# Projecting two z2 row blocks inside the last four segments of a memory-transformer and gMLP kernel

## The chip, the core and the metric

The kernel runs on one NeuronCore of a Trainium2 chip. The core has a matrix engine (TensorE, PE), which writes its results to PSUM, a vector engine (VectorE, DVE), a scalar engine (ScalarE, ACT), a general engine (GpSimd, POOL), and a queue engine (SyncE, SP), which here only issues transfers. The engines run at the same time and wait for each other through semaphores. The metric is the time of one execution on the device in microseconds, the median over several executions.

## The reference

Two parts follow each other on a sequence of 2048 tokens with 512 features. The first is attention with a recurrent memory, in segments of 32 tokens (64 segments), each with 8 memory tokens that come out of the segment before. The second is a gated MLP (gMLP).

```python
for s in range(n_seg):                      # 64 segments, one after the other
    h = concatenate([mem, x_norm[segment]]) # 8 + 32 tokens
    q, k, v = h @ Wq, h @ Wk, h @ Wv        # 32 heads of 128
    o = softmax(q @ k.T * scale + mask) @ v
    o = o @ Wo
    mem = o[:, :8]; outs.append(o[:, 8:])
h = x + concatenate(outs)

z  = gelu(layernorm(h) @ w_in)              # 512 -> 1792
z1 = z[..., :896]
z2 = layernorm(z[..., 896:])
g  = w_sp @ z2 + b_sp                       # mixing over the 2048 tokens
out = h + (z1 * g) @ w_out
```

The weights are bf16, and so is the output.

## The kernel before

**Order.** Every operation is recorded in program order by a small emitter (`em.add`), which derives the semaphore waits from named tokens for what an operation reads and writes. Each engine then runs its own operations strictly in that order; there is no scheduler. A token `("ps", b)` stands for one of the eight PSUM banks.

**The recurrence** is the loop over `s` from line 913. In a segment TensorE projects q, k and v (`QK`, `V_half`; the matmuls are recorded by the helper `mm` at L289 and L290), scores them (`S_half`), ACT computes the exponentials, the logarithm and the reciprocal (`sm_exp` L608, `sm_ln` L626, `sm_rcp` L630), DVE normalises (`sm_norm` L634), TensorE multiplies with V (`PV_half`, L666 and L672), ACT and DVE copy the result out (`cT_evac`, L686 and L688), and TensorE multiplies with Wo (`Wo`, L701). ACT copies that to `part` (`part_evac`, L713), and `mem_out` (L722, L728, L730) turns its first 8 rows into the memory of the next segment. `mask_dve` (L585) puts the mask into PSUM once a segment on DVE.

Matmuls with 32 tokens use only 32 columns of the array. They are issued in groups of four, in four column tiles (`tile_position=(0, 32 * c)`), which run at the same time; the profile writes such a matmul as 128*32.

**Filler places.** There are two lists of work that doesn't depend on the segment in hand. `gx` has groups of five steps: four with four matmuls each (one for each 128 of the 512 features) into PSUM bank 3 (`XB`), and one that copies the result out. Each segment takes one group (line 999). Two steps stand ahead of `PV_half`, two behind it, and the copy stands behind the copies of `cT`:

```python
        fill(nw1)
        for f in xs[:2]:
            f()
        PV_half(s, 0)
        PV_half(s, 1)
        for f in xs[2:4]:
            f()
        fill(nw2)
        cT_evac(0, "act", (0,))
```

`gx` holds 60 groups, for keys, queries and values of later memory rows, and so the segments 60 to 63 have none. The other list, `wq`, holds the output projection of the memory rows of the four segments before (`WoX_mm`, L751), and the sums `F_group` (L736) and `WoX_scatter` (L761), which put the rows of four segments together in one block of 128 tokens. Where a segment has a group of `gx`, `wq` gives `nw1` pieces ahead of it and none in the middle; where it has none, it gives one ahead and the others in the middle.

**Where the recurrence ends.** After segment 63 the loop over `rb` from line 1167 makes the gMLP's inputs, one block of 128 tokens at a time. For each block, `z2_mm` projects two halves of 448 columns (`HF`) with four matmuls each (L1108), and ACT applies GELU from PSUM (L1111). `z2_norm` and `z2_apply` normalise on DVE and POOL (L1121 to L1132). From block 2 on, two groups of z1 are projected in each block (`z1_group`, L1139), with GELU on ACT (L1142), and from block 4 on five matmuls of the mixing (`mix`, L1146). The PSUM banks 5 to 7 go round through `zbank()`.

Into the first blocks the rest of the recurrence is woven: the last `F_group(15)` between the halves of block 0, 32 matmuls `WoX_mm` behind it, `WoX_evac` (L756) on ACT, and `WoX_scatter`, `F_add` (L741) and `h_done` in block 1. `F_add(14)`, the same sum for the block before, is the last operation of the loop over segments on DVE. `xn2_apply` (L774) normalises the token blocks 14 and 15 in the blocks 1 and 2, and TensorE transposes them (L1190) in the blocks 2 and 3, with a copy by DVE (L1104).

**Transfers around it.** SP issues them in order: in segments 48 to 51 the second half of `w_in` (`w_in2`), from segment 49 on the transposed token blocks (`xn2T_dma`), in segment 63 the first 512 tokens of the mixing weights (`load_wT(0)`, L907), then the first half of `w_in` (`w_in1`, L974), the bias (L975) and six transposed blocks (L788); behind them `h_done`'s store (L771), more mixing weights, `w_out`, and the 16 blocks of h.

Of the kernel before, what the change touches and what calls it, by code (L numbers as in the profile page):

```python
# [9 lines left out]
ACT = mybir.ActivationFunctionType  # L10
# [168 lines left out]
def fast_path(nc, st, keep, A_x, A_mem0, A_Wq, A_Wk, A_Wv, A_Wo, A_seg_len, B_w_in, B_w_sp, B_b_sp, B_w_out, out):  # L179
# [8 lines left out]
    RB = S // 128  # L188
    DC = D // 128
    F = B_w_in.shape[1]  # L190
    FH = F // 2
# [15 lines left out]
    def sb(name, shape, dt):  # L207
        return st.enter_context(nc.sbuf_tensor("f_" + name, shape, dt))
# [5 lines left out]
    def region(off, n):  # L214
        return arena[:, off:off + n]
# [21 lines left out]
    Vs = sb("Vs", [128, 2, 512], BF)  # L237
# [5 lines left out]
    xn = sb("xn", [128, 2, 512], BF)  # L243
# [28 lines left out]
    ps = st.enter_context(nc.psum_tensor("f_ps", [128, 8, 512], F32))  # L272
# [5 lines left out]
    def PB(b):  # L278
        return ("ps", b)

    def sp(fn, **k):
        return em.add("sp", fn, dma=True, **k)

    def pe(fn, **k):
        return em.add("pe", fn, **k)
# [9 lines left out]
    def act(fn, **k):  # L295
        return em.add("act", fn, **k)

    def dve(fn, **k):
        return em.add("dve", fn, **k)
# [234 lines left out]
    XB = 3  # L534
# [198 lines left out]
    def F_group(rb, bank):  # L733
        for j in range(4):
            i = (4 * rb + j) % 8
            pe(lambda e, i=i, j=j: e.matmul(ps[32 * j:32 * j + 32, bank, :], lhsT=F_sb[:, :], rhs=part[:, i, :], start=True, stop=False,  # L736
                                            tile_position=(0, 32 * j)),
               reads=[("part", i, 0), ("part", i, 1), "F"], writes=[PB(bank)])

    def F_add(rb, bank):  # L740
        dve(lambda e: e.tensor_tensor(out=hbuf[:, rb % 2, :], in0=ps[:, bank, :], in1=hbuf[:, rb % 2, :], op=ALU.add),  # L741
            reads=[PB(bank), ("h", rb % 2)], writes=[("h", rb % 2)])
# [4 lines left out]
    def WoX_mm(rb, qr, bgs=range(8)):  # L747
        for bg in bgs:
            b, g = bg // 4, bg % 4
            h = 16 * b + 4 * qr + g  # L750
            pe(lambda e, h=h, g=g, i=8 * qr + bg: e.matmul(ps[32 * g:32 * g + 32, WXB, :], lhsT=cTx[:, rb % 2, i, :], rhs=w_o[:, h, :],  # L751
                                                           start=(i < 4), stop=(i >= H - 4), tile_position=(0, 32 * g)),
               reads=[("cTx", rb % 2), ("Wo", h // 8)], writes=[PB(WXB)])

    def WoX_evac(rb):
        act(lambda e: e.activation(out=partx[:], in_=ps[:, WXB, :], func=ACT.Copy), reads=[PB(WXB)], writes=["partx"])  # L756

    def WoX_scatter(rb, bank):
        for c in range(4):
            q = slice(32 * c, 32 * c + 32)  # L760
            pe(lambda e, q=q, c=c: e.matmul(ps[q, bank, :], lhsT=Sc[:, q], rhs=partx[:], start=False, stop=True, tile_position=(0, 32 * c)),  # L761
               reads=["partx", "Sc"], writes=[PB(bank)])
# [10 lines left out]
    def xn2_apply(rb, j):  # L773
        dve(lambda e: e.tensor_scalar(out=xo[:, j, :], in0=hbuf[:, rb % 2, :], scalar1=mv[:, rb, 0:1], scalar2=rstd[:, rb:rb + 1],  # L774
                                      op0=ALU.subtract, op1=ALU.mult),
            reads=[("h", rb % 2), ("mv", rb), ("rstd", rb)], writes=[("xo", j)])
# [5 lines left out]
    w_in2 = region(4 * WSZ, WH).rearrange("p (dc f) -> p dc f", dc=DC)  # L782
    w_in1 = region(4 * WSZ + QX, WH).rearrange("p (dc f) -> p dc f", dc=DC)
    xts = [region(4 * WSZ + i * QX + WH, 8 * D).rearrange("p (r dc t) -> p r dc t", r=8, dc=DC) for i in range(2)]
# [94 lines left out]
    gx = []  # L879
# [7 lines left out]
    for ck in range(1, 4):  # L887
        for n in range(4 if ck == 1 else 0, 8):
            vx_group(ck, n)
        for r in range(4):  # L890
# [2 lines left out]
                    qkx_group(ck, mi, r, b)  # L893


    wTb = [region(0, RB * 512).rearrange("p (t sc c) -> p t sc c", sc=RB, c=64),
           region(3 * WSZ, RB * 512).rearrange("p (t sc c) -> p t sc c", sc=RB, c=64)]
    h_sb = region(RB * 512, RB * D).rearrange("p (rb d) -> p rb d", rb=RB)
# [2 lines left out]
    z2 = region(2 * WSZ, RB * FH).rearrange("p (rb f) -> p rb f", rb=RB)  # L901
# [3 lines left out]
    def load_wT(tb, after):  # L905
        for t in range(8):
            sp(lambda e, t=t: e.dma_start(wTb[tb % 2][:, t, :, :], wT_d[8 * tb + t]), reads=[("wTd", 8 * tb + t)],  # L907
               writes=[("wT", tb % 2, t)], after=after)
# [4 lines left out]
    for s in range(NSEG):  # L913
        j4 = s % 4
        rb = s // 4
# [154 lines left out]
        if 3 * CK <= s < 3 * CK + 4:  # L1070
            dc = s - 3 * CK
# [7 lines left out]
    lastQ, lastK, lastV = lastop["q"], lastop["k"], lastop["v"]  # L1079
# [1 line left out]

    TB = 512
    NTB = S // TB
    HF = FH // 2
    em.mark_const("w_in1", "w_out", *[("w_in2", dc) for dc in range(DC)])

    def xT2(rb):
        return xts[rb // 8][:, rb % 8, :, :]
# [13 lines left out]
    def xn_copy(rb, j, bank):  # L1102
        src = psb[:, bank, 0:512].rearrange("p (dc c) -> p dc c", dc=DC)
        dve(lambda e: e.tensor_copy(out=xT2(rb), in_=src), reads=[PB(bank)], writes=[("xn2T", rb)], after=[lastop["s"], lastop["x"]])  # L1104

    def z2_mm(rb, hf, bank):
        for dc in range(DC):
            pe(lambda e, dc=dc: e.matmul(ps[:, bank, 0:HF], lhsT=xT2(rb)[:, dc, :], rhs=w_in2[:, dc, hf * HF:(hf + 1) * HF],  # L1108
                                         start=(dc == 0), stop=(dc == DC - 1)),
               reads=[("w_in2", dc), ("xn2T", rb)], writes=[PB(bank)])  # L1110
        act(lambda e: e.activation(out=z2[:, rb, hf * HF:(hf + 1) * HF], in_=ps[:, bank, 0:HF], func=ACT.Gelu_apprx_tanh),  # L1111
            reads=[PB(bank)], writes=[("z2", rb, hf)], after=[lastV])

    st2 = sb("st2", [128, 2, 2, 6], F32)
    mv2 = sb("mv2", [128, 2, 2], F32)
# [2 lines left out]
    def z2_norm(rb):  # L1118
        j = rb % 2
        for hf in range(2):  # L1120
            dve(lambda e, hf=hf: e.bn_stats(out=st2[:, j, hf, :], in_=z2[:, rb, hf * HF:(hf + 1) * HF]), reads=[("z2", rb, hf)],  # L1121
                writes=[("st2", j, hf)])
# [36 lines left out]
    def zbank():  # L1159
        zcnt[0] += 1  # L1160
        return 5 + zcnt[0] % 3
# [3 lines left out]
    ACC = (0, 1, 2, 3, 4)  # L1165
    LAG = 4
    for rb in range(RB):
        z2_mm(rb, 0, zbank())
        if rb == 0:
            F_group(RB - 1, XB)  # L1170
        z2_mm(rb, 1, zbank())
        if rb == 0:
            for qr in range(4):
                WoX_mm(RB - 1, qr)
            endA = em.by_eng["pe"][-1]
            WoX_evac(RB - 1)
            load_wT(1, [endA])
            sp(lambda e: e.dma_start(w_out, B_w_out.rearrange("(fb p) d -> p fb d", p=128)), writes=["w_out"], after=[endA])
        if rb == 1:
            WoX_scatter(RB - 1, XB)  # L1180
            F_add(RB - 1, XB)
            h_done(RB - 1)
            for r in range(RB):
                sp(lambda e, r=r: e.dma_start(h_sb[:, r, :], h_d[r]), reads=[("hd", r)], writes=[("hs", r)], after=[lastQ])
        if rb in (1, 2):
            xn2_apply(RB - 3 + rb, rb % 2)
        if rb in (2, 3):
            r, j, bank = RB - 4 + rb, (rb - 1) % 2, zbank()
            for dc in range(DC):
                pe(lambda e, dc=dc, j=j, bank=bank: e.transpose(out=psb[:, bank, dc * 128:(dc + 1) * 128], in_=xo[:, j, dc * 128:(dc + 1) * 128],  # L1190
                                                                identity=ident[:, :]), reads=[("xo", j), "ident"], writes=[PB(bank)])
            xn_copy(r, j, bank)
        z2_norm(rb)
        if rb > 0:
            z2_apply(rb - 1)
        for _ in range(2):
            if rb >= 2 and z1list and (z1list[0][0] < 3 or rb >= 12):
                tb, fb = z1list.pop(0)
                z1_group(tb, fb, zbank())
        if rb == 8:  # L1200
            check_rows()
        if rb >= LAG:
            for fb, bk in enumerate(ACC):
                mix(0, fb, rb - LAG, bk)
# [33 lines left out]
    for tb in range(NTB):  # L1238
        for fb in range(len(ACC) if tb == 0 else 0, FB):
            if tb == 0:  # L1240
                bank = 5 + fb % 3
            else:
                bank = MB[mcnt % 3]
# [19 lines left out]
    for d0 in (0, 256):  # L1263
        bank = 7 if d0 else 5
# [9 lines left out]
def general_path(nc, st, keep, A_x, A_mem0, A_Wq, A_Wk, A_Wv, A_Wo, A_seg_len, B_w_in, B_w_sp, B_b_sp, B_w_out, out):  # L1274
# [23 lines left out]
    if True:  # L1298
# [51 lines left out]
        def PB(b):  # L1350
            return ("ps", b)
# [423 lines left out]
        if True:  # L1775
# [24 lines left out]
            wspr = B_w_sp.rearrange("(tk p) s -> p tk s", p=128)  # L1800
            HF = FH // 2
            tstate = {"cnt": 0, "banks": (4, 5)}
# [40 lines left out]
            def z2_mm(rb, hf):  # L1843
                bank = 2 + hf
                for dc in range(DC):
                    em.add("pe", lambda e, dc=dc: e.matmul(
                        ps[:, bank, 0:HF], lhsT=xn2T[:, dc, rb * 128:(rb + 1) * 128], rhs=w_in[:, dc, FH + hf * HF:FH + (hf + 1) * HF],
                        start=(dc == 0), stop=(dc == DC - 1)),
                        reads=["w_in", ("xn2T", rb)], writes=[PB(bank)])

            def z2_gelu(rb, hf):
                bank = 2 + hf
                em.add("act", lambda e: e.activation(
                    out=z2[:, rb, hf * HF:(hf + 1) * HF], in_=ps[:, bank, 0:HF], func=ACT.Gelu_apprx_tanh),
                    reads=[PB(bank)], writes=[("z2", rb)])
# [175 lines left out]
```

The softmax here doesn't subtract the row's maximum and nothing guards it: scores larger than these inputs give would overflow.

## Time and profile before

| what | us |
|---|---|
| median of 5 executions | 856.29 |
| lowest and highest | 855.45, 858.59 |
| the profiled execution, its own time | 856.26 |
| its span, from the first to the last instruction | 854.5 |

The mean granted TensorE clock of the profiled execution is 0.998. Its span in four stretches, as the view by stretches of time gives them (busy us of each engine):

| stretch, us from the start | what runs | PE | DVE | ACT | POOL |
|---|---|---|---|---|---|
| 607.73 to 617.46 | segment 57, with a filler | 9.71 | 5.93 | 6.60 | 1.69 |
| 646.64 to 656.37 | segment 61, without | 9.11 | 5.32 | 6.13 | 1.69 |
| 675.85 to 693.34 | end of the recurrence, first gMLP blocks | 16.77 | 12.49 | 10.69 | 5.28 |
| 693.34 to 852.50 | the rest | 156.34 | 70.69 | 25.71 | 11.28 |

In the profile, L and a number is a line of the kernel before. A row of the timeline has the start, the length, the engine, the line, the operation, what it writes and reads, and in brackets how long the engine had been idle and which operation it waited for. The ends of matmuls are modelled, so the distance between two starts says more than the length of one row. The copies of the mask, L585, come once a segment and serve as a mark for how long a segment takes.

### The profile page before, as it was taken

The page shows a single profiled execution, that of the slowest core. Times are in us where ns is not written, and L with a number is a line of the kernel's source. Part 1 is how long each engine was busy: PE and PEld are TensorE (multiplying, and loading weights), DVE is VectorE, ACT ScalarE, POOL GpSimd, SP SyncE. Part 2 cuts the span into 40 slices and gives each one's busy share as a digit, 9 for nine tenths or more (in the row PEclk, how much of TensorE's full clock was granted, in tenths as well). Part 3 has the DMA queues.
Part 4 walks back from the last instruction along what each step waited for, and adds up shares of the span by engine and source line. Part 5 has one row for each costly group of instructions (what it writes and reads, how often), then busy time and mean ns, then how long its engine had stood idle before and what let it go on. Part 6 is the DMA issues. An engine that isn't in the chain of part 4 may idle for free.

```text
span 854.5 us, 45967 instructions
## 1 busy us (share of the span) xinstructions
PE 836.1 (98%) x22497; PEld 440.9 (52%) x19432; DVE 513.3 (60%) x1318; ACT 472.4 (55%) x1367; POOL 169.0 (20%) x425
## 2 busy tenths in 40 slices
PE   8889999999999999999999999999999999999997
PEld 8545555555555555555555555555455444444443
DVE  3446666676766666666767666666666554453443
ACT  3446666766667666667666676766676655400000
POOL 7312212121211122121212111212112232100000
PEclk9999999999999999999999999999999999999999
DMA  9972222222332222312223423343321780033001
GB/s 324 390 218 77 68 66 35 60 72 60 77 91 64 42 65 42 78 34 60 68 63 77 91 62 73 74 78 80 60 48 50 205 265 1 1 111 107 30 13 41
DMA packets 112922, 75.27 MB, mean 88 GB/s; under 512 B 70728, under 2 KB 98512, under 8 KB 112720
## 3 DMA queue, kind: packets, MB, share of 16 engines
q1 hardware_dynamic: 111504, 70.88, 30.8%
q8 instruction: 166, 2.72, 1.4%
q0 software_dynamic: 384, 1.05, 0.3%
q10 hardware_dynamic: 832, 0.33, 0.1%
q14 instruction: 36, 0.29, 0.1%
HBM read 39.46 MB, written 20.58 MB: 70 GB/s over the span
## 4 chain that ended last, share of the span: by engine, by line
PE 92%; SPq 3%; DMA 2%; DVE 1%; issue 1%; ACT 1%; ACTq 0%
PE f_ps L289 33%; PE f_ps L701 14%; PE f_ps L290 12%; PE f_ps L1146 11%; PE f_ps L751 3%; PE f_ps L666 3%; PE f_ps L1220 3%; PE f_ps L1108 3%; PE f_ps L1139 3%; PE f_ps L498 2%; SPq L329 2%; DMA f_arena<-in_A_Wk_dram 2%; PE f_ps L595 1%; PE f_ps L615 1%; PE f_ps L672 1%
## 5 line engine op out<-in xcount | busy, mean ns | idle before, releaser
L289 PE MATMUL f_ps<-f_arena,f_hT 128*32 128x512 bf16 (+1 forms) x5632 | 360.4, 331 | 0.2
L289 PEld LDWEIGHTS f_ps<-f_arena,f_hT 128*32 128x32 bf16 x5632 | 134.9, 96 | 160.2 <-issue 69.4
L290 PE MATMUL f_ps<-f_arena,f_hT 128*32 128x512 bf16 (+1 forms) x2560 | 189.2, 315 | 0.0
L559 ACT ACTIVATE f_Tst<-f_ps 128x512 bf16<-128x512 f32 (+1 forms) x320 | 149.6, 510 | 57.7 <-PE f_ps L289 54.1
L701 PE MATMUL f_ps<-f_arena,f_cT 128*32 128x256 bf16 x4096 | 131.7, 276 | 1.4 <-ACT f_cT L686 0.8
L638 POOL TENSOR_TENSOR f_E_sb<-f_R_sb,f_E_sb 128x64 bf16<-128x64 f32 x128 | 57.0, 445 | 361.6 <-ACT f_R_sb L630 361.6
L567 DVE STREAM_TRANSPOSE f_QT<-f_Tst 128x256 uint32<-128x256 uint32 x128 | 57.0, 446 | 94.8 <-ACT f_Tst L559 94.8
L701 PEld LDWEIGHTS f_ps<-f_arena,f_cT 128*32 128x32 bf16 x4096 | 91.2, 95 | 38.4 <-ACT f_cT L686 22.1
L1146 PE MATMUL f_ps<-f_arena 128*128 128x512 bf16 x448 | 100.6, 379 | 0.0
L688 DVE TENSOR_SCALAR f_cT<-f_ps 128x160 bf16<-128x160 f32 x256 | 65.1, 316 | 35.7 <-PE f_ps L672 35.7
L713 ACT ACTIVATE f_part<-f_ps 128x256 bf16<-128x256 f32 x128 | 49.2, 384 | 60.0 <-PE f_ps L701 56.0
L658 DVE TENSOR_SCALAR f_V_sb<-f_ps 128x512 bf16<-128x512 f32 (+1 forms) x128 | 71.0, 555 | 13.7 <-PE f_ps L289 13.7
L686 ACT ACTIVATE f_cT<-f_ps 128x160 bf16<-128x160 f32 x256 | 57.1, 309 | 36.8 <-PE f_ps L672 36.8
L1146 PEld LDWEIGHTS f_ps<-f_arena 128*128 128x128 bf16 x448 | 43.8, 98 | 52.7
L567 DVE STREAM_TRANSPOSE f_KT<-f_Tst 128x128 uint32<-128x128 uint32 (+1 forms) x192 | 65.8, 356 | 2.7
L626 ACT ACTIVATE f_R_sb<-f_ps 128x160 f32<-128x160 f32 x128 | 39.0, 305 | 34.8 <-PE f_ps L290 32.9
L634 DVE TENSOR_TENSOR f_E_sb<-f_R_sb,f_E_sb 128x160 bf16<-128x160 f32 x128 | 41.6, 325 | 23.4 <-ACT f_R_sb L630 23.4
L1152 DVE TENSOR_TENSOR f_arena<-f_ps,f_arena 128x512 f32<-128x512 f32 x28 | 19.3, 690 | 54.4 <-PE f_ps L1146 52.4
L289 PE MATMUL f_ps<-f_arena,f_hTe 128*32 128x512 bf16 x640 | 48.8, 382 | 0.0
L608 ACT ACTIVATE f_E_sb<-f_ps 128x224 bf16<-128x224 f32 x128 | 45.8, 358 | 0.0
L751 PE MATMUL f_ps<-f_arena,f_cTx 128*32 128x512 bf16 x512 | 43.8, 379 | 0.0
L630 ACT ACTIVATE f_R_sb<-f_R_sb 128x160 f32<-128x160 f32 x128 | 42.6, 333 | 2.0
(117 smaller groups left out, 1024.6 us busy)
## 6 DMA issues: line engine op xcount, KB each, us to landing
wT_d<-f_wst SPq DMA_DIRECT2D x32, 256.0 KB
f_arena<-wT_d SPq DMA_DIRECT2D x32, 256.0 KB
f_arena<-in_A_Wv_dram SPq DMA_DIRECT2D x4, 1024.0 KB
f_arena<-in_A_Wk_dram SPq DMA_DIRECT2D x4, 1024.0 KB
f_arena<-in_A_Wo_dram SPq DMA_DIRECT2D x4, 1024.0 KB
f_Vx<-vext_d SPq DMA_DIRECT2D x124, 32.0 KB
f_arena<-in_A_Wq_dram SPq DMA_DIRECT2D x3, 1024.0 KB
vext_d<-f_Vs SPq DMA_DIRECT2D x20, 128.0 KB
```

Of the source, the lines that this page charges most:

```text
L289: return e.matmul(out, lhsT=lhsT, rhs=rhs, start=start, stop=stop, skip_group_check=True, tile_position=pos)
L290: return e.add_instruction(mybir.InstMatmult(name=nc.get_next_instruction_name(), engine=mybir.EngineType.PE, ins=[e.lower_ap(rhs), e.lowe ...
L559: act(lambda e: e.activation(out=st_.rearrange("p (hp i r) -> p hp i r", i=32, r=2), in_=ps[:, bank, 0:64 * np_].rearrange("p (hp r i) -> ...
L567: dve(lambda e: e.transpose(out=dst, in_=src), reads=tok, writes=[(nm, b, k) for k in halves(b, p0, np_)])
L638: pool(lambda e: e.tensor_tensor(out=ev, in0=rv, in1=ev, op=ALU.mult), reads=[("R", b), ("Ex", b)], writes=[("Ex", b)])
L658: dve(lambda e: e.tensor_scalar(out=dst, in0=src, scalar1=VSC, scalar2=None, op0=ALU.mult), reads=[PB(bank)], writes=tok)
L686: act(lambda e: e.activation(out=dst, in_=src, func=ACT.Copy, scale=UNSC), reads=[PB(PVB[c])], writes=tok)
L688: dve(lambda e: e.tensor_scalar(out=dst, in0=src, scalar1=UNSC, scalar2=None, op0=ALU.mult), reads=[PB(PVB[c])], writes=tok)
L701: pe(lambda e, h=h, g=g, i=i, b=b, c=c: e.matmul(ps[32 * g:32 * g + 32, bank, 0:d1 - d0], lhsT=cTh[:, i, 8:40], rhs=w_o[:, h, d0:d1], star ...
L713: act(lambda e: e.activation(out=part[:, s % 8, d0:d1], in_=ps[:, bank, 0:d1 - d0], func=ACT.Copy), reads=[PB(bank)], writes=[("part", s % ...
L751: pe(lambda e, h=h, g=g, i=8 * qr + bg: e.matmul(ps[32 * g:32 * g + 32, WXB, :], lhsT=cTx[:, rb % 2, i, :], rhs=w_o[:, h, :], start=(i < 4 ...
L1146: pe(lambda e: e.matmul(ps[:, bank, 0:TB], lhsT=z2[:, sc, fb * 128:(fb + 1) * 128], rhs=wTb[tb % 2][:, :, sc, :], start=(sc == 0), stop=(s ...
```

## The change

The list `gx` gets four more groups, one for each half of the row blocks 0 and 1 of z2. They are taken by the segments 60 to 63. A group has sixteen matmuls in four column tiles instead of four full ones; DVE copies its 448 columns as bf16, ahead of GELU, into buffers that the recurrence has no more use for by then (`Vs` and `xn`). Behind the recurrence, the loop over blocks has for row blocks 0 and 1 only the GELU, which ACT now reads from these buffers, ahead of all others. `F_group(15)` and `WoX_mm` follow directly on the recurrence; `WoX_scatter`, `F_add` and `h_done` move from block 1 to block 2, `xn2_apply` from blocks 1 and 2 to 2 and 3, and the transposes from blocks 2 and 3 to 4 and 5. As the last four segments have groups now, the pieces of `wq` in segments 60 and 62 are taken two at a time ahead of `PV_half`.

```diff
+    HF = FH // 2
+
+    def zs(i):
+        return ((Vs, xn)[i // 2][:, i % 2, 0:HF], (("Vs", "xn")[i // 2], i % 2))
+
+    def z2_group(rb, hf):
+        t, tok = zs(2 * rb + hf)
+
+        def step(dc):
+            for c in range(4):
+                pe(lambda e, c=c: e.matmul(ps[32 * c:32 * c + 32, XB, 0:HF], lhsT=xts[rb // 8][:, rb % 8, dc, 32 * c:32 * c + 32],
+                                           rhs=w_in2[:, dc, hf * HF:(hf + 1) * HF], start=(dc == 0), stop=(dc == DC - 1),
+                                           tile_position=(0, 32 * c)),
+                   reads=[("w_in2", dc), ("xn2T", rb)], writes=[PB(XB)])
+
+        gx.append([lambda dc=dc: step(dc) for dc in range(DC)] +
+                  [lambda: dve(lambda e: e.tensor_copy(out=t, in_=ps[:, XB, 0:HF]), reads=[PB(XB)], writes=[tok])])
+
+    for rb in range(2):
+        for hf in range(2):
+            z2_group(rb, hf)
...
+    def z2_act(rb, hf):
+        t, tok = zs(2 * rb + hf)
+        act(lambda e: e.activation(out=z2[:, rb, hf * HF:(hf + 1) * HF], in_=t, func=ACT.Gelu_apprx_tanh), reads=[tok],
+            writes=[("z2", rb, hf)], after=[lastV])
...
     for rb in range(RB):
-        z2_mm(rb, 0, zbank())
+        for hf in range(2):
+            if rb < 2:
+                z2_act(rb, hf)
+            else:
+                z2_mm(rb, hf, zbank())
         if rb == 0:
             F_group(RB - 1, XB)
-        z2_mm(rb, 1, zbank())
-        if rb == 0:
             for qr in range(4):
                 WoX_mm(RB - 1, qr)
...
-        if rb == 1:
+        if rb == 2:
             WoX_scatter(RB - 1, XB)
             F_add(RB - 1, XB)
             h_done(RB - 1)
...
-        if rb in (1, 2):
-            xn2_apply(RB - 3 + rb, rb % 2)
         if rb in (2, 3):
-            r, j, bank = RB - 4 + rb, (rb - 1) % 2, zbank()
+            xn2_apply(RB - 4 + rb, rb % 2)
+        if rb in (4, 5):
+            r, j, bank = RB - 6 + rb, rb % 2, zbank()
```

More of the change, by code (lines that the diff above doesn't have):

```diff
@@ L1083, in fast_path @@
     NTB = S // TB
-    HF = FH // 2
     em.mark_const("w_in1", "w_out", *[("w_in2", dc) for dc in range(DC)])
```

## The prediction

> **What bounds the kernel now.** I read the page's busy table first, then TensorE's timeline in two segments of the recurrence (one with a filler, one without), then the timelines around the place where the recurrence ends and the gated MLP begins, and last the chain of waits there.
>
> ```profile
> PE 836.1 (98%) x22497; PEld 440.9 (52%) x19432; DVE 513.3 (60%) x1318; ACT 472.4 (55%) x1367; POOL 169.0 (20%) x425
> ```
>
> PE is busy 98% of the span, but that share hides two kinds of stage. TensorE's timeline in segment 57, which has a filler (columns: start in us, length, engine, line, operation, count, idle before):
>
> ```profile
> 613.54 0.39 PE L751 MATMUL f_ps<-f_arena,f_cTx 128*32 128x512 bf16 x4
> 613.76 0.60 PE L289 MATMUL f_ps<-f_arena,f_hTe 128*32 128x512 bf16 x8
> 614.29 0.27 PE L666 MATMUL f_ps<-f_E_sb,f_V_sb 32*128 32x40 bf16 x16
> ...
> 614.93 0.61 PE L289 MATMUL f_ps<-f_arena,f_hTe 128*32 128x512 bf16 x8
> 615.38 1.73 PE L701 MATMUL f_ps<-f_arena,f_cT 128*32 128x256 bf16 x56
> ```
>
> and the same place in segment 61, which has none:
>
> ```profile
> 652.46 0.39 PE L751 MATMUL f_ps<-f_arena,f_cTx 128*32 128x512 bf16 x4
> 652.78 0.54 PE L666 MATMUL f_ps<-f_E_sb,f_V_sb 32*128 32x40 bf16 x16
> ...
> 653.54 0.27 PE L666 MATMUL f_ps<-f_E_sb,f_V_sb 32*128 32x40 bf16 x16 [0.19 <-DVE f_E_sb L634]
> ...
> 654.29 1.73 PE L701 MATMUL f_ps<-f_arena,f_cT 128*32 128x256 bf16 x56 [0.38 <-ACT f_cT L686]
> ```
>
> From the L751 row to the L701 row it is 1.84 us in segment 57 and 1.83 us in segment 61. The filler's sixteen matmuls take no time: where they are missing, TensorE waits instead (0.38 us for the cT copy, 0.19 us for the normalised scores, and the first L666 group stretched from 0.27 to 0.54 us). The chain of waits says the same of a segment without filler: ACT L626 and L630, DVE L634, PE L666, ACT L686, PE L701. So the last four segments, 60 to 63, are set by the softmax chain, with idle TensorE time inside. After them TensorE sets the pace:
>
> ```profile
> 675.85 0.47 PE L761 MATMUL f_ps<-f_partx,f_Sc 128*32 128x512 bf16 x4
> 676.25 0.93 PE L1108 MATMUL f_ps<-f_arena 128*128 128x448 bf16 x4
> 677.11 0.40 PE L736 MATMUL f_ps<-f_part,f_F_sb 128*32 128x512 bf16 x4
> 677.45 0.93 PE L1108 MATMUL f_ps<-f_arena 128*128 128x448 bf16 x4
> 678.31 1.91 PE L751 MATMUL f_ps<-f_arena,f_cTx 128*32 128x512 bf16 x32
> 680.15 1.69 PE L1108 MATMUL f_ps<-f_arena 128*128 128x448 bf16 x8
> 681.77 0.40 PE L761 MATMUL f_ps<-f_partx,f_Sc 128*32 128x512 bf16 x4
> 682.10 1.69 PE L1108 MATMUL f_ps<-f_arena 128*128 128x448 bf16 x8
> 684.23 0.40 PE L1190 MATMUL f_ps<-f_ident,f_xo 128*128 128x128 bf16 x4 [0.44 <-DVE f_xo L774]
> 684.46 1.89 PE L1139 MATMUL f_ps<-f_arena 128*128 128x512 bf16 x8
> 686.63 1.69 PE L1108 MATMUL f_ps<-f_arena 128*128 128x448 bf16 x8 [0.28 <-DVE f_arena L1104]
> ```
>
> The reader sees L1108 (the z2 projection) four times at full price, two waits on DVE (0.44 and 0.28 us), and from 686.63 on none: between there and the end the list of TensorE's waits is empty. Time taken out ahead of 693.34, where L1146 (the mixing) starts, comes off the end.
>
> **What the change takes from that place.** Sixteen matmuls of 128x448 (row blocks 0 and 1). By the starts above: 676.25 to 677.11 and 677.45 to 678.31 are 0.86 us each, 680.15 to 681.77 is 1.62: together 3.34 us (0.19 us a matmul is 3.0; the rest comes with the change of tile shape around each group).
>
> **What is then late.** Two things had been hidden by the removed groups. F_group(15) (L736) reads the last segment's part, and now follows directly on the scatter; the copy that it needs is the first row here (ACT's timeline, then DVE's):
>
> ```profile
> 676.14 0.38 ACT L713 ACTIVATE f_part<-f_ps 128x256 bf16<-128x256 f32 x1 [0.49 <-PE f_ps L701]
> 676.54 1.28 ACT L1163 ACT_TABLE_LOAD   x1
> ```
> ```profile
> 676.36 0.69 DVE L741 TENSOR_TENSOR f_hbuf<-f_ps,f_hbuf 128x512 bf16<-128x512 f32 x1 [1.88 <-PE f_ps L761]
> ```
>
> So L736 starts at about 676.57 (L713 ends at 676.52, and L701 starts 0.05 us after the L686 copy it needs) and ends its turn 0.22 later, at 676.8. The 32 WoX matmuls (L751) write the PSUM bank that F_add(14), the DVE row, reads until 677.05. In the old order they came 1.26 us after that; now they wait for it, to 677.12. Everything on PE behind them waits too. Then, by old durations: L751 1.84 to 678.96, z2 block 2 (L1108 x8) 1.62 to 680.58, scatter 0.33 to 680.91, and the first z1 group (L1139), which stood at 684.46.
>
> **Is its weight there?** w_in1 is the next limit: SP issues it at 673.61, behind 2.1 MB of mixing weights. In the trace's DMA records the packets of 1,792 bytes (896 bf16, a row of w_in1) run to 680.44, and the queue's semaphore is complete at 680.88. So z1 starts at 680.93 at the earliest: the cover that was 3.6 us is used up, and costs about nothing now; it would cost all that the transfer is later.
>
> **The rest of the stage.** The transposes of row blocks 14 and 15 (L1190) move from blocks 2 and 3 to blocks 4 and 5 with xn2_apply two blocks ahead of them, so both DVE waits go (0.72 us). From 680.93: two z1 groups 1.73, z2 1.51, z1 1.73, z2 1.51, transposes 0.23, z1 1.73 put the first mixing at 689.37; the second transposes, which the old order had done by then, add 0.23: 689.60 against 693.34. **Gain 3.74 us.** As a sum: 3.34 + 0.72, and about 0.3 back for the new waits and tile changes.
>
> ACT's queue: table load to 677.82, two GELUs from SBUF, WoX_evac, two GELUs, then z2 block 2. Two GELUs back to back take 1.12 us here (L1111, from PSUM), so WoX_evac runs from 678.96+ to 679.7, and the scatter behind it is due at 680.58. [...] Block 2's GELUs come at 681.3 and 681.9, and the second z1 group needs the first's bank at 681.8: just hidden, 0 to 0.1 us. DVE must finish the norm of blocks 0 and 1 before F_add(15): free at about 682.1, transposes of block 14 wanted at 687.4. POOL's queue keeps its order. No DMA is added; SP is busy with six transposes until 684.8 in any case, so the second weights, w_out and the h loads behind them don't move.
>
> **What the change puts into segments 60 to 63.** Each gets sixteen matmuls of 128x32 weights by 448 columns in four column tiles, half of them ahead of L666, half ahead of L701, and one DVE copy of 448 f32 from PSUM. Nearest rows: sixteen L289 with 512 columns start at 640.63 and the next group at 641.49, 0.86 us; times 448/512 is 0.75 us. The copy: 0.62 us, as L585 (448 wide, from SBUF) and a little under L658 (512 wide, PSUM, 0.69). It sits between the cT copies and the small hT copy (L728), where DVE idles 1.12 us in segment 62. Below nothing is excluded (work is added to a chain that waits for none of it); above, 0.75 on PE and 0.62 on DVE, both in the chain, is 1.37 us a segment. I take the measured middle: segments 36 to 43 have just this filler (sixteen such matmuls of 512 columns and a DVE copy of 512). The distance between the mask copies (L585) of neighbouring segments is 9.72 to 9.73 us for 60 to 62, 9.73 to 9.74 for 57 to 59, and 9.73 to 9.93 for 36 to 43, mostly 9.73. Over all filled segments the mean is some 0.08 us above 9.72 because of single stalls of 0.1 to 0.8 us, which the waits list partly as "issue". So four segments cost 4 x 0.08 = **0.3 us**, bounds 0 and 0.8 (two stalls of 0.4). In segments 60 and 62 a WoX step also moves from behind L666 to ahead of it (0.22 us); 56 and 58 already have it there.
>
> [...]
>
> **Sum.** Profiled execution 856.26 us (span 854.5): 856.26 - 3.74 + 0.3 = 852.8; its time is the median's within 0.03, so 852.9.
>
> **Rivals.** Changes within 0.2% (1.71 us) count as none here.
> - *Filler paid in full on PE* (no change): 4 x 0.75 = 3.0 back, 855.6. For it: PE is 98% busy. Against it: 57 and 61 take equally long. Chance 0.08.
> - *Filler in series with the recurrence* (slower): the DVE copy waits for the last z2 matmul, and hT's copy, which releases the next segment, waits behind it; with the matmuls 4 x 1.37 = 5.5, 858.0. It decides from a segment of 9.73 + 0.93 = 10.66 us on, where the gain is gone; slower by 0.2% from 11.1. For it: the place in DVE's order. Against: segments 36 to 43. Chance 0.05.
> - *w_in1 late*: the bytes issued up to it share queues with others; 1.5 us later gives 854.4. For it: no slack is left. Against: nothing new is issued. Chance 0.07, still faster.
> - The forecast: 0.80; its own range 852.0 to 854.2.
> That the change doesn't move the work is no rival: in the built order the sixteen matmuls stand in the four segments and are gone behind them.
>
> Range 851.6 to 855.0: the forecast's bounds (no stall and an early w_in1 below), the late w_in1 above. Faster 0.86, same 0.09, slower 0.05.
>
> **What would show it.** Mask copies 9.7 to 9.9 us apart in segments 60 to 62; after the scatter a wait of some 0.3 to 0.5 us before L736 and one on F_add before the 32 WoX matmuls; the first z1 group about 3.5 us earlier against the scatter, with at most a short wait for DMA; no wait at the transposes. A segment of 10.5 us, or a wait over 1 us at z1, would prove me wrong.

## The result, and the profile after

| | kernel before | changed kernel |
|---|---|---|
| median, us | 856.46 (43 executions) | 854.0 (22 executions) |
| lowest and highest | 853.68, 859.26 | 852.22, 856.81 |
| profiled execution, its span | 854.5 | 853.4 |

The ratio of the times is 0.9972 with a 95% interval of 0.9963 to 0.9981: 2.4 us faster (1.6 to 3.2). A second comparison gave 0.9961 (0.9949 to 0.9973), 3.3 us. The forecast was 852.9, 3.4 us faster.

TensorE's timeline of the changed kernel in segment 61, the place that was shown with waits before:

```profile
654.24 0.39 PE L751 MATMUL f_ps<-f_arena,f_cTx 128*32 128x512 bf16 x4
654.46 0.55 PE L906 MATMUL f_ps<-f_arena 128*32 128x448 bf16 x8
654.94 0.27 PE L666 MATMUL f_ps<-f_E_sb,f_V_sb 32*128 32x40 bf16 x16
...
655.63 0.56 PE L906 MATMUL f_ps<-f_arena 128*32 128x448 bf16 x8
656.08 1.74 PE L701 MATMUL f_ps<-f_arena,f_cT 128*32 128x256 bf16 x56
```

L906 is the new z2 group. From L751 to L701 it is 1.84 us, as in the segments with and without a filler before (1.84 and 1.83). Both waits in brackets are gone, and the first L666 group is back at 0.27 us: the sixteen matmuls fill what had been waiting. The mask copies of segments 60 to 62 (DVE's timeline, first before, then after) stand 9.73 and 9.72 us apart in both:

```profile
646.51 0.62 DVE L585 CAST f_ps<-f_mask 128x448 f32<-128x448 bf16 x1
656.24 0.62 DVE L585 CAST f_ps<-f_mask 128x448 f32<-128x448 bf16 x1
665.96 0.62 DVE L585 CAST f_ps<-f_mask 128x448 f32<-128x448 bf16 x1
```
```profile
648.30 0.62 DVE L585 CAST f_ps<-f_mask 128x448 f32<-128x448 bf16 x1
658.03 0.62 DVE L585 CAST f_ps<-f_mask 128x448 f32<-128x448 bf16 x1
667.75 0.62 DVE L585 CAST f_ps<-f_mask 128x448 f32<-128x448 bf16 x1
```

Behind the recurrence, TensorE's timeline (z2 is L1129 now, z1 L1165, the transposes L1218, the mixing L1172):

```profile
677.31 0.39 PE L761 MATMUL f_ps<-f_partx,f_Sc 128*32 128x512 bf16 x4
677.52 0.83 PE L736 MATMUL f_ps<-f_part,f_F_sb 128*32 128x512 bf16 x4
678.50 1.91 PE L751 MATMUL f_ps<-f_arena,f_cTx 128*32 128x512 bf16 x32
680.34 1.69 PE L1129 MATMUL f_ps<-f_arena 128*128 128x448 bf16 x8
681.96 0.40 PE L761 MATMUL f_ps<-f_partx,f_Sc 128*32 128x512 bf16 x4
683.20 1.90 PE L1165 MATMUL f_ps<-f_arena 128*128 128x512 bf16 x8 [0.84 <-DMA f_arena<-in_B_w_in_dram]
...
689.69 0.39 PE L1218 MATMUL f_ps<-f_ident,f_xo 128*128 128x128 bf16 x4
689.91 1.89 PE L1165 MATMUL f_ps<-f_arena 128*128 128x512 bf16 x8
691.64 1.24 PE L1172 MATMUL f_ps<-f_arena 128*128 128x512 bf16 x5
```

From the scatter to the mixing it is 14.33 us, and 14.55 with the second transposes, which now come later; before it was 17.49 with both. The waits at the transposes are gone. One wait is new: 0.84 us for w_in1 ahead of the first z1 group. The WoX matmuls start at 678.50, and the DVE row that they wait for is

```profile
677.75 0.69 DVE L741 TENSOR_TENSOR f_hbuf<-f_ps,f_hbuf 128x512 bf16<-128x512 f32 x1 [0.96 <-PE f_ps L761]
```

which ends at 678.44.

**A warning on whole spans.** The profiled span fell by only 1.1 us, although the stretch gained 2.9. The mask copy of segment 59, which the change comes after, stands at 636.79 in the trace of before and at 638.57 in that of after. In the traces of all kernels here it lies between 634.50 and 639.92, though nothing ahead of it differs: the 59 distances from the first mask copy to this one add up to between 3.7 and 8.2 us more than 59 times the usual 9.725. So two traces are compared here from the mask copy of segment 62 on, and the medians carry these stalls as noise of a microsecond or so.

### The profile page after: what moved, and what is told of

Read it like the earlier page. It is cut to its first block, busy times and chain, and to the rows that moved or that the text cites. A ratio compares the mean times of both kernels' runs of the same rounds, so it can differ in the third digit from the quotient of the medians.

```text
span 853.4 us, 46065 instructions
## 1 busy us (share of the span) xinstructions
PE 835.9 (98%) x22545; PEld 441.3 (52%) x19480; DVE 515.1 (60%) x1322; ACT 471.6 (55%) x1367; POOL 168.6 (20%) x425
## 3 DMA queue, kind: packets, MB, share of 16 engines
q8 instruction: 166, 2.72, 1.4%
## 4 chain that ended last, share of the span: by engine, by line
PE 91%; DMA 3%; SPq 3%; issue 1%; ACT 1%; DVE 0%; ACTq 0%
PE f_ps L289 33%; PE f_ps L701 14%; PE f_ps L290 12%; PE f_ps L1172 11%; PE f_ps L751 3%; PE f_ps L666 3%; PE f_ps L1165 3%; PE f_ps L1248 3%; PE f_ps L1129 2%; PE f_ps L498 2%; SPq L329 2%; DMA f_arena<-in_A_Wk_dram 2%; PE f_ps L595 1%; PE f_ps L615 1%; DMA f_arena<-in_B_w_in_dram 1%
## 5 line engine op out<-in xcount | busy, mean ns | idle before, releaser
L289 PE MATMUL f_ps<-f_arena,f_hT 128*32 128x512 bf16 (+1 forms) x5632 | 360.8, 331 | 0.3
L289 PEld LDWEIGHTS f_ps<-f_arena,f_hT 128*32 128x32 bf16 x5632 | 134.4, 96 | 161.3 <-issue 69.4
L701 PE MATMUL f_ps<-f_arena,f_cT 128*32 128x256 bf16 x4096 | 132.2, 275 | 0.8 <-issue 0.6
L701 PEld LDWEIGHTS f_ps<-f_arena,f_cT 128*32 128x32 bf16 x4096 | 91.6, 95 | 38.3 <-ACT f_cT L686 21.6
L1172 PE MATMUL f_ps<-f_arena 128*128 128x512 bf16 x448 | 100.6, 379 | 0.0
L1172 PEld LDWEIGHTS f_ps<-f_arena 128*128 128x128 bf16 x448 | 43.7, 98 | 52.8
L289 PE MATMUL f_ps<-f_arena,f_hTe 128*32 128x512 bf16 x640 | 49.0, 382 | 0.0
L751 PE MATMUL f_ps<-f_arena,f_cTx 128*32 128x512 bf16 x512 | 43.6, 379 | 0.1
```

What stands on the lines that cost most here:

```text
L289: return e.matmul(out, lhsT=lhsT, rhs=rhs, start=start, stop=stop, skip_group_check=True, tile_position=pos)
L701: pe(lambda e, h=h, g=g, i=i, b=b, c=c: e.matmul(ps[32 * g:32 * g + 32, bank, 0:d1 - d0], lhsT=cTh[:, i, 8:40], rhs=w_o[:, h, d0:d1], star ...
L1172: pe(lambda e: e.matmul(ps[:, bank, 0:TB], lhsT=z2[:, sc, fb * 128:(fb + 1) * 128], rhs=wTb[tb % 2][:, :, sc, :], start=(sc == 0), stop=(s ...
```

## The experiments

The columns of the table are the ratio to the kernel before with its interval, and four distances from each kernel's trace: between the mask copies of segments 60 to 62 (two), and from the mask copy of segment 62 to the first z1 group and to the first mixing. In the kernels with the old order behind the recurrence both transposes come ahead of the mixing, in those with the new order one (0.22 us). Where z1 waited for w_in1, the wait stands in brackets.

| kernel | ratio (95%) | segments | to z1 | to mixing |
|---|---|---|---|---|
| before | 1 | 9.73, 9.72 | 18.50 | 27.38 |
| changed | 0.9972 (0.9963 to 0.9981) | 9.73, 9.72 | 15.45 (0.84) | 23.89 |
| after_again | 0.9961 (0.9949 to 0.9973) | 9.73, 9.73 | 15.60 (0.99) | 24.04 |
| fill_only | 0.9998 (0.9982 to 1.0015) | 9.72, 9.73 | 18.09 | 26.90 |
| no_fill | 0.9946 (0.9926 to 0.9967) | 9.73, 9.72 | 15.31 (0.59) | 23.75 |
| no_fill_again | 0.9971 (0.9958 to 0.9983) | 9.73, 9.72 | 15.09 (0.47) | 23.53 |
| fill_double | 0.9998 (0.9985 to 1.0010) | 10.11, 10.32 | 16.37 | 24.82 |
| win1_first | 0.9963 (0.9952 to 0.9975) | 9.73, 9.72 | 14.81 | 23.25 |
| before_win1_first | 1.0006 (0.9990 to 1.0023) | 9.73, 9.72 | 18.08 | 26.96 |
| win1_late | 1.0000 (0.9985 to 1.0014) | 9.73, 9.72 | 17.21 (2.13) | 25.65 |
| wox_first | 0.9970 (0.9956 to 0.9984) | 9.72, 9.73 | 14.43 | 22.87 |
| both_first | 0.9971 (0.9958 to 0.9983) | 9.72, 9.73 | 15.26 | 23.70 |
| both_first_again | 0.9968 (0.9954 to 0.9983) | 9.72, 9.73 | 15.53 | 23.97 |
| both_calm | 0.9964 (0.9952 to 0.9976) | 9.73, 9.73 | 15.41 | 24.13 |

### What do the fillers cost?

**fill_only** adds the four groups to the kernel before and nothing else:

```diff
...
+    for rb in range(2):
+        for hf in range(2):
+            z2_group(rb, hf)
```

> The kernel before, with the four z2 groups added to segments 60 to 63; their results are not used, and z2 of blocks 0 and 1 is projected again behind the recurrence as before. My theory (the groups lie in waits of TensorE): 0 to 0.3 us slower than before, mask copies of segments 60 to 62 9.72 to 9.75 us apart. Paid in full on TensorE: 3.0 us slower, 10.5 us apart. In series with the recurrence: 5.5 us slower, 11.1 us apart.

Measured: 0.9998, and segments of 9.72 and 9.73 us. The groups cost nothing that can be measured. Paid in full they would have made 1.0035 (3.0 us of 857), in series 1.0064 (5.5 us); both lie outside the interval.

**no_fill** takes the same three lines out of the changed kernel.

> The changed kernel without the four groups: the z2 projection of blocks 0 and 1 is left out altogether, and the GELU reads what lies in the buffers. My theory: 0 to 0.3 us faster than the changed kernel (ratio to before about 0.997), segments 60 to 62 at 9.72 us, and behind the recurrence the same picture with a wait of some 0.8 us for w_in1. Fillers paid in full: 3.0 us faster than the changed kernel (ratio 0.9937).

Measured: 0.9946, an interval that overlaps the changed kernel's but has its middle 2.2 us lower, while the segments in the trace are the same. So it ran again beside the changed kernel:

> The changed kernel without the four groups (z2 of blocks 0 and 1 left out), once more, because its first ratio (0.9946) lay 2.2 us below the changed kernel's, with overlapping intervals, while its trace had segments of the same length. My theory (fillers free): the same as the changed kernel within 0.3 us. If the fillers cost something that the traces of segments 60 to 62 don't show: 2 to 3 us faster than the changed kernel beside it.

> The changed kernel once more. If its gain is the 2.8 us that the traces show from segment 62 on, less what varies from run to run ahead of it: ratio to before 0.9967 to 0.9972, and a wait at the first z1 group of 0.3 to 1.2 us, as w_in1's last packet has come 13.9 to 14.9 us after the mask copy of segment 62 so far. If the 0.84 us was an accident of one execution: no such wait.

Measured: no_fill 0.9971, changed kernel 0.9961. The difference has turned round, so the first one was not repeated and lies within what the medians vary by. From the mask copy of segment 62 to the mixing the kernels without fillers take 23.75 and 23.53 us, those with them 23.89 and 24.04. Less its own wait for w_in1, each takes 23.16 and 23.06 without fillers, and 23.05 twice with them: the filler in the last segment costs nothing either.

**fill_double** asks how much room there is, by issuing each filler matmul twice:

```diff
...
-        gx.append([lambda dc=dc: step(dc) for dc in range(DC)] +
+        gx.append([lambda dc=dc: (step(dc, 0), step(dc, 1)) for dc in range(DC)] +
```

> The changed kernel with each filler matmul issued twice into the same sum, so z2 of blocks 0 and 1 comes out doubled. A group takes 1.5 us instead of 0.75. If the room in a segment is the 0.87 us that I read from segments 57 to 61: 0.6 us more a segment, mask copies of 60 to 62 about 10.35 us apart, 2.5 us slower than the changed kernel. If there is more room: segments stay at 9.73 and the time doesn't change. If the single filler is already paid: 0.75 a segment, 3.0 us slower.

Measured: mask copies 10.32 us apart in the step to segment 60, 10.11 to 61, 10.32 to 62:

```profile
648.86 0.62 DVE L585 CAST f_ps<-f_mask 128x448 f32<-128x448 bf16 x1
658.97 0.62 DVE L585 CAST f_ps<-f_mask 128x448 f32<-128x448 bf16 x1
669.29 0.62 DVE L585 CAST f_ps<-f_mask 128x448 f32<-128x448 bf16 x1
```

That is 0.59 and 0.38 us more than 9.73; segment 61 has one WoX step (0.22 us) fewer ahead of the multiplication with V. A doubled group of 1.50 us (twice 0.75) less the 0.59 that shows leaves 0.91 us of room, where 0.87 was read (in the timelines of before, segment 57's filler takes 0.53 and 0.45 us by the starts, and its L751 row 0.22 where segment 61's has 0.32: together 0.88). The free place is real, and it is full. The ratio is 0.9998, as if the whole gain were given back, but it proves less than the mask copies do: of the 2.5 us by which this trace is longer from the mask copy of segment 59 to the mixing, 1.20 us is a pause of TensorE in the Wo matmuls of segment 63, of a kind that comes up again below.

### What takes the missing part?

**win1_first** issues w_in1 ahead of the mixing weights:

```diff
         if s == NSEG - 1:
-            load_wT(0, [lastop["q"]])
...
             sp(lambda e: e.dma_start(w_in1, winr[:, :, 0:FH]), writes=["w_in1"], after=[lastop["s"], lastop["x"]])
+            load_wT(0, [lastop["q"]])
```

> The changed kernel with the w_in1 transfer issued ahead of the first 512 tokens of mixing weights in segment 63. If the wait for w_in1 is what took a part of my gain: the 0.84 us wait ahead of the first z1 group goes, 0.8 us faster than the changed kernel (ratio to before about 0.9963), no new wait at the mixing, which comes at 691. If the transfer is only shifted and the mixing weights come too late instead, or if the missing part lies elsewhere: no change against the changed kernel (0.9972).

TensorE's timeline of this kernel from the scatter on (z2 is L1128, z1 L1164):

```profile
675.48 0.39 PE L761 MATMUL f_ps<-f_partx,f_Sc 128*32 128x512 bf16 x4
675.69 0.83 PE L736 MATMUL f_ps<-f_part,f_F_sb 128*32 128x512 bf16 x4
676.66 2.19 PE L751 MATMUL f_ps<-f_arena,f_cTx 128*32 128x512 bf16 x32
678.78 1.69 PE L1128 MATMUL f_ps<-f_arena 128*128 128x448 bf16 x8
680.40 0.40 PE L761 MATMUL f_ps<-f_partx,f_Sc 128*32 128x512 bf16 x4
680.73 1.47 PE L1164 MATMUL f_ps<-f_arena 128*128 128x512 bf16 x6
```

z1 follows the scatter without a wait, and no wait comes at the mixing. It gains 0.64 us to z1 and to the mixing against the changed kernel, not 0.84, because the WoX matmuls take 2.12 us here (676.66 to 678.78) instead of 1.84, for a reason that comes below. In the medians (0.9963 beside 0.9972 and 0.9961) so little can't be told.

**before_win1_first** is the same reordering on the kernel before.

> The kernel before with the same reordering of the w_in1 transfer. My theory: w_in1 had 3.6 us of cover there, so nothing changes (within 0.2 us, ratio 1.000). If the order of these transfers is worth something by itself: about 0.8 us faster (0.999).

Measured: 1.0006, as before. The order of the transfers is worth something (0.64 us in the trace) only where z1 comes early.

**win1_late** puts the bias ahead of w_in1 in the changed kernel:

```diff
-            sp(lambda e: e.dma_start(w_in1, winr[:, :, 0:FH]), writes=["w_in1"], after=[lastop["s"], lastop["x"]])
             sp(lambda e: e.dma_start(bsp_b, ...
+            sp(lambda e: e.dma_start(w_in1, winr[:, :, 0:FH]), writes=["w_in1"], after=[lastop["s"], lastop["x"]])
```

> The changed kernel with the bias transfer (0.52 MB) issued ahead of w_in1. If w_in1's landing now sets when z1 starts: 0.52 MB at the 390 GB/s of that stretch is 1.3 us more of waiting, 1.3 us slower than the changed kernel (ratio to before about 0.9987). If the 0.84 us wait belongs to one execution only and is slack in others: 0.5 us slower or less.

The list of TensorE's waits of this kernel, from 640 us on, has one row (columns: engine and line, waited for, us in total, times, longest):

```profile
PE f_ps L1165 <- DMA f_arena<-in_B_w_in_dram: 2.1, 1, 2.1
```

The wait has grown by 1.1 to 1.3 us against the changed kernel's 0.84 and 0.99, near the 1.3 us expected for 0.52 MB. z1 and the mixing come 1.6 to 1.8 us later, because the landing does: w_in1's last packet comes 16.58 us after the mask copy of segment 62, 1.5 to 1.7 us later than in the changed kernel (14.92 and 15.12). The wait itself grew by less, since WoX took 2.31 us in this execution and TensorE came to z1 later. The ratio is 1.0000 with the expected 0.9987 inside its interval. So w_in1's landing sets the start of z1.

### Is there more behind it?

**wox_first** and **both_first** put the 32 WoX matmuls ahead of F_group(15), in a bank that nobody reads by then:

```diff
...
-            F_group(RB - 1, XB)
             for qr in range(4):
-                WoX_mm(RB - 1, qr)
+                WoX_mm(RB - 1, qr, bank=OB)
             endA = em.by_eng["pe"][-1]
-            WoX_evac(RB - 1)
+            WoX_evac(RB - 1, OB)
+            F_group(RB - 1, XB)
```

> The changed kernel with the 32 WoX matmuls ahead of F_group(15), in PSUM bank 2, so that they wait neither for F_add(14) nor for the last part copy. If w_in1's landing sets the start of z1: TensorE's pause of 0.75 us goes, and the wait for w_in1 grows by the same 0.75 to 1.6 us; same time as the changed kernel (ratio 0.997). If the pause counts by itself: 0.75 us faster (0.9963).

> w_in1 ahead of the mixing weights and WoX ahead of F_group(15), both on the changed kernel. If they are two limits one behind the other: 0.84 + 0.75 = 1.6 us faster than the changed kernel (ratio to before about 0.9953), more than w_in1 alone by 0.75. If only one counts: as w_in1 alone.

wox_first missed what I expected: z1 came at 14.43 with no wait for w_in1. In this execution w_in1's last packet came 13.89 us after the mask copy of segment 62, where the others with this order had 14.48 (before), 14.92 (changed), 15.12 (after_again), 14.84 (fill_only), 14.83 and 14.73 (no_fill twice) and 14.09 (fill_double). The landing varies by over a microsecond, and the interval of wox_first (0.9956 to 0.9984) holds both answers; the run decides nothing.

both_first has w_in1 early (its last packet at 9.68) and should have shown the 1.6 us. It didn't: z1 comes at 15.26. So it ran once more:

> The changed kernel with w_in1 ahead of the mixing weights and WoX ahead of F_group(15), once more, because its profile had one pause of 1.1 us in the WoX matmuls listed as issue. If such pauses come and go: no pause or a short one this time, 1 to 1.6 us faster than the changed kernel beside it. If this order brings the pause on: the same pause in the same place, and no gain.

TensorE's timeline of the second run:

```profile
673.24 0.39 PE L761 MATMUL f_ps<-f_partx,f_Sc 128*32 128x512 bf16 x4
673.46 1.03 PE L751 MATMUL f_ps<-f_arena,f_cTx 128*32 128x512 bf16 x15
675.87 1.24 PE L751 MATMUL f_ps<-f_arena,f_cTx 128*32 128x512 bf16 x17 [1.38 <-issue]
```

The pause is back, behind the same fifteenth matmul, 1.38 us after 1.11 us: WoX begins at once and stops in the middle, and the profile names nothing that it waited for (that is what "issue" means there). wox_first has it too, at the same matmul, with 0.26 us. Is it the 2.1 MB of mixing weights that run beside it? **both_calm** issues them, the bias and the six transposed blocks behind WoX:

```diff
             endA = em.by_eng["pe"][-1]
...
+            load_wT(0, [endA])
+            sp(lambda e: e.dma_start(bsp_b, ...
+            for r in range(8, RB - 2):
+                xn2T_dma(r, [lastop["s"], lastop["x"]])
             load_wT(1, [endA])
```

> As both_first, with the mixing weights, the bias and the six transposed blocks issued behind WoX instead of in segment 63, so that little but w_in1 moves while the recurrence ends. If the issue pauses of TensorE in that stretch come from the transfers beside it (2.1 MB at 390 GB/s): no pause from segment 63 to the scatter, 0.3 to 1 us faster than both_first, and the mixing weights still land ahead of the mixing. If the pauses have nothing to do with these transfers: the same as both_first. If the weights come too late now: a wait at the first mixing, slower.

```profile
674.91 1.03 PE L751 MATMUL f_ps<-f_arena,f_cTx 128*32 128x512 bf16 x15
677.21 1.24 PE L751 MATMUL f_ps<-f_arena,f_cTx 128*32 128x512 bf16 x17 [1.26 <-issue]
```

The first of the mixing weights' packets comes 14.30 us after the mask copy here, behind the pause, and the pause is 1.26 us all the same. So the mixing weights are not its cause. The w_in1 transfer still ran until 11.26 in this run, into the pause, and is not excluded by it.

What the pauses go with can be read from the transfer records. A queue of the kind "instruction" moves blocks of 16,384 bytes, 166 of them in an execution of the changed kernel. In these three runs one starts at 9.54, 9.69 and 9.64 us after the mask copy and takes 1.0 to 1.1 us, and the matmuls go on 1.3 to 1.5 us after its end. In the changed kernel that block starts at 8.25 and 8.83, and the wait for F_add(14) ends at 10.75, so that such a pause has no room to show.

Nor does the pause belong to WoX. In the three runs, and in wox_first, it stands ahead of the 21,728th matmul of the execution. In win1_first and win1_late the same number is the twelfth matmul of WoX, and there the pause is the 0.28 and 0.47 us by which WoX was longer. In fill_double it is the twentieth of the 64 Wo matmuls of segment 63, the 1.20 us noted above. In the kernel before a pause stands 128 matmuls earlier, which is also the twentieth of Wo (first row before, second fill_double):

```profile
674.63 1.47 PE L701 MATMUL f_ps<-f_arena,f_cT 128*32 128x256 bf16 x45 [0.16 <-issue]
679.40 1.47 PE L701 MATMUL f_ps<-f_arena,f_cT 128*32 128x256 bf16 x45 [1.20 <-issue]
```

In all 14 traces together, 96 pauses of TensorE of more than 0.08 us are listed as issue from 60 us on. Each of them ends 1.2 to 1.9 us after the end of such a block, 90% of them 1.24 to 1.57 us after it, although the blocks start some 4 us apart (median). So these pauses go with the arrival of instruction blocks. That is a coincidence in time in every case, and no run moved a block; why a block comes late stays open.

No version with a measurable advantage over the changed kernel came out: all that remove one of its waits lie between 0.9963 and 0.9971.

## Why the prediction was right

**The fillers cost nothing: right, and better than the sum.** The step compared segments 57 and 61, found the same length with and without a filler, and took 0.3 us for stalls. Shown: 9.72 to 9.73 us in every trace with a single filler, and fill_only at 0.9998. The term should have been 0: the stalls of the filled segments are real, but they don't come from the filler. That these 0.3 us were charged for nothing is luck for the total, since they stand against a wait that was left out (below). The two rivals that make it pay are excluded by fill_only and fill_double.

**F_group and WoX wait: right.** The prediction had WoX 1.27 us after the scatter, behind F_add(14); it is 678.50 less 677.31, 1.19. The scatter behind z2 block 2 was due 4.73 us after the first (680.58 less 675.85); it is 4.65 (681.96 less 677.31).

**w_in1: the step that was mis-sized.** The prediction said that "z1 starts at 680.93 at the earliest", that the cover "is used up, and costs about nothing now". In distances from the scatter that is 5.08 us; it was 5.89, and 0.84 of it is the wait. TensorE was ready after 5.05, so all of the miss is the transfer. z1 stands 2.72 us earlier against the scatter than before (8.61 less 5.89), where about 3.5 was expected. Two things were taken as fixed that are not. The landing was read once, and its last packet varies from 13.89 to 15.12 us after the mask copy. And it was set against a scatter which in that one trace came 9.89 us after the mask copy, where every other trace of a single filler or none has 9.56 to 9.61: TensorE's pause in the Wo matmuls of segment 63 (the row at 674.63 above), which the transfer did not share, had given it 0.33 us more time. The repeat shows 0.99 us, so the wait is a part of the change, not an accident. I had it as a rival, "w_in1 late", with a chance of 0.07; at 0.8 to 1.0 us it lies between that rival's 1.5 and the forecast's 0, and the 0.99 us is barely under the 1 us that was to prove the forecast wrong.

**The transposes and the rest: right.** Both DVE waits are gone, TensorE has no wait from 640 us on but the one for w_in1, and from z1 to the mixing it is 8.44 us (683.20 to 691.64), as predicted (680.93 to 689.37). The four GELUs from SBUF hid behind the WoX matmuls and z2: WoX_evac ran from 680.46, the scatter at 681.96 waited for nothing. Two of them, reading bf16 from SBUF, took 1.03 to 1.04 us back to back, and the next two, reading f32 from PSUM, 0.96: 0.04 us more for each, off the path. (The 1.12 us that the prediction read for two from PSUM has a wait in it: the second starts 0.57 us after the first there, 0.43 here.) The 0.75 us that the prediction scaled from the L289 row for a filler's matmuls (0.215 us for four column tiles of 512 columns together, no more than the 0.216 of one full-width z1 matmul of 512) came out: in fill_double sixteen matmuls of 448 columns in four tiles, ahead of L701, start at 646.18 and the next group at 646.95, 0.77 us.

**The sum.** Predicted 3.74 less 0.3, 3.4 us. In the traces 17.49 less 14.55, 2.9 us, and 0 for the segments. Two more traces of the old order, fill_only and before_win1_first, have 17.34 and 17.40 us between the same marks, and the repeat of the new one 14.70: 2.6 to 2.9. The medians say 2.4 and 3.3. The forecast of 852.9 lies 1.1 us under the median. The 0.8 to 1.0 us at z1, less the 0.3 us charged for the fillers, make 0.5 to 0.7 of that; the rest lies within the interval of the ratio, which is 0.8 us to either side.

## What to carry to other kernels

Whether a loop has free time on an engine that is busy 98% is read by comparing two of its rounds, one with more work and one with less: if they are equally long, the difference is the room, and it can be filled up to there and no further (here 1.84 and 1.83 us from L751 to L701; 0.87 us of room was read, and fill_double left 0.91). When work is taken out ahead of a transfer's first use, the landing must be taken from several runs and against a mark that the transfer shares, because a cover of 3.6 us that shrinks to nothing is then ruled by the spread of the landing (here 13.89 to 15.12 us after the mask copy). And behind a wait that is removed the next can stand: here a PSUM bank (WoX starts 0.06 us after F_add(14), its reader), a weight's landing (0.84 and 0.99 us of waiting) and the pauses of TensorE that go with the instruction blocks (0.26 to 1.38 us at WoX) lay within a microsecond or so of each other.

## What the hardware showed that I had not expected

- From 60 us on, TensorE paused for up to 1.4 us with no operation to wait for. The pause near the end of the recurrence stands at the same matmul, counted from the start of the execution, in every kernel with fillers that shows it (the 21,728th) and 128 earlier in the kernel before, whatever operation it falls in, and all 96 pauses in 14 traces end 1.2 to 1.9 us after a 16,384-byte block of the instruction queue.
- The unchanged 59 segments varied by 4.5 us in sum from trace to trace (3.7 to 8.2 us over the usual length), mostly in single stalls, the longest of 1.7 us (fill_only, 469.05 to 480.50 us, with two of the issue pauses in it, of 0.64 and 0.75 us). That is more than the whole effect of this change, and intervals from medians of 11 to 22 executions are 0.8 to 1.8 us wide to either side.
- Where the tile shape changed, TensorE took about 0.1 us more: in the changed kernel eight matmuls of 128x448 with a 32-column group behind them took 1.62 us (680.34 to 681.96), with full-width ones behind them 1.52 (684.93 to 686.45, 688.17 to 689.69).
